# A larger allowance between engines in the list schedule of a Fourier, MoE and channel-mix kernel

## The chip, the cores and the metric

The kernel runs on one core of a Trainium2 chip. The time is microseconds (us) of device time of one execution. TensorE (PE in the profile) multiplies matrices into PSUM; VectorE (DVE) and ScalarE (ACT) do everything elementwise; SyncE (SP) and GpSimd (POOL) only start DMAs here. The program gives each engine its own list of instructions; an instruction that needs the result of another engine waits for a semaphore.

## The reference, cut to what matters

The input x has 4 batches of 3072 tokens with 256 channels, in float32.

```
X  = rfft(x, axis=1)
Yr = Xr @ w_r - Xi @ w_i + b_r ;  Yi = Xr @ w_i + Xi @ w_r + b_i
Y  = sign(Y) * max(|Y| - 0.01, 0)          (real and imaginary part apart)
x  = irfft(Y)                               stage 1
h  = x @ w_in ; x = (h - tanh(h)) @ w_out   stage 2, 256 -> 2048 -> 256
xk = mu_k*x + (1-mu_k)*x_prev ; xr likewise with mu_r
k  = max(xk @ w_k, 0) ; v = (k*k) @ w_v     stage 3, 256 -> 1024 -> 256
out = sigmoid(xr @ w_r2) * v
```

## The kernel before

Every float32 operand of a matmul is cut into a high and a low part, and each product is three matmuls: high by high, low by high, high by low. The cut costs one ScalarE copy (L345) and one VectorE subtraction (L348) for each tile.

Stage 1 does the transform in two steps per batch, with a trip through DRAM between them: first-step matmuls into PSUM banks `a`, 12 units per batch that take `q` tiles back from DRAM, a matmul into bank `g`, one into bank `y` with the weights, the threshold on VectorE (L529 to L534), the cut into `zh` and `zl`, a matmul into bank `v`, and so on.

Stage 2 goes over 24 chunks of 512 tokens and, within a chunk, 8 pieces of the hidden width (`reg_pair`, "a pair" below). The first matmul of a pair is done with seven products of half size instead of eight (`reg_h`). Two of the banks named `g` take three of them: ScalarE copies each result out (`p2`, `p5`, `p3`, L796). The other four go, one after the other, into one bank named `y` or `a` in turn (`m` in the code): each product adds to what the bank already holds, and after each of the first three an add on VectorE (L799, `hs<-y,p` or `hs<-a,p`) reads the bank. So the next product into that bank may only start when the add before it has read. Then ScalarE makes tanh (L839), VectorE subtracts (L840), both cut the result into `gh` and `gl` (L345, L348), and PE takes these with 6 matmuls of 512 columns for each half into the two banks `v`. Two banks stand behind each name, so PE always has several pairs under way.

Stage 3 goes over the 24 chunks again (`reg_m2`): four pieces of the same seven-product form, all with bank `y` for `m`; the square on VectorE (L968) or ScalarE; 12 matmuls of 256 columns for each piece into `v`; and four groups of 6 matmuls into bank `a` for the gate (`a<-wh,yh` and so on), each read by a sigmoid on ScalarE (L1003).

None of this is in the order in which the loops stand. The code only registers operations with an engine, a duration by formula, a priority and what they depend on; `_Plan.run` then makes a list schedule on a clock of its own, and the instructions are emitted in the order of the planned starts. On each engine the planner takes, among the operations that are ready at that time, the one of lowest priority number, and an operation is ready when all that it depends on have ended, plus an allowance where the other operation ran on another engine:

```
        for x in lst:
            if gated:
                t = o.start + 1e-3
            elif x.eng == o.eng == "pe":
                t = o.end
            else:
                t = o.end + o.lat
```

The allowance `o.lat` is `SEM` for everything but DMAs. It is in nanoseconds and only shapes the order: no instruction waits for it on the chip. The planner's durations for what is spoken of below are 3 x 119 for a product, `n * 1.042 + 69` for a VectorE operation with two inputs of n columns (336 for an add of 256), `n * 0.833 + 93` for a ScalarE operation from SBUF.

Of the kernel before, what the change touches and what calls it, by code (L numbers as in the profile page):

```python
# [142 lines left out]
    __slots__ = ("eng", "dur", "lat", "emit", "deps", "prio", "creates", "users", "nleft", "start", "end", "idx", "ready", "frees", "nbytes")  # L143


SEM = 130


class _Plan:
# [5 lines left out]

    def op(self, eng, dur, emit, prio, writes=(), reads=(), after=(), lat=SEM, seq=True, nbytes=0):
        o = _Op()
        o.nbytes = nbytes
        o.eng, o.dur, o.emit, o.prio, o.lat = eng, dur, emit, prio, lat
        o.idx = len(self.ops)  # L160
        o.start = o.end = None
        deps = set(after)
        o.creates, o.frees = [], []
        for t in reads:
            deps.update(t.writers)
            t.readers.append(o)
        for t in writes:
            if not t.writers:
                o.creates.append(t)
                if t.tag is not None:  # L170
                    self.rings.setdefault((t.pool, t.tag), []).append(t)
            elif seq:
                deps.add(t.writers[-1])
            else:
                deps.add(t.writers[0])
            t.writers.append(o)
            deps.update(r for r in t.readers if r is not o)
        for t in list(reads) + list(writes):
            if t.pool is not None:
                t.pool.ops.append(o)  # L180
        deps.discard(o)
        o.deps = deps
        self.ops.append(o)
        return o
# [867 lines left out]
```

## Time and profile before

| | us |
|---|---|
| median of 3 runs | 2008.94 |
| the three runs | 2005.75 to 2009.99 |
| the profiled execution | 2006.93 |
| its span, first to last instruction | 2005.1 |
| PE busy in the span | 1961.8 |
| VectorE busy | 1599.4 |
| ScalarE busy | 1476.9 |

The profiled execution lies 2.0 below the median of the runs. Stage 1 takes the first 350 us or so, stage 2 goes to about 1400, stage 3 to the end. PE is the engine that is nearly always busy, so the table alone says little of where time is lost. The end of a matmul is modelled in the profile and matmuls overlap (rows of 0.28 us start 0.12 apart), so a busy PE may still start its matmuls late. What tells it is the distance between the starts of neighbouring matmuls, and the length of a row: a matmul that was held up inside PE shows a longer row than its neighbours of the same shape.

### The profile page before, as it was taken

How to read it: one execution, taken by the hardware profiler on the slowest of the kernel's cores; microseconds unless marked ns; L12 is line 12 of the kernel's file. 1: busy time of each engine (PE TensorE's matmuls, PEld its weight loads, DVE VectorE, ACT ScalarE, POOL GpSimd, SP SyncE). 2: the span in 40 equal slices, each digit the busy share in tenths (PEclk: the TensorE clock that was granted, in tenths of full speed). 3: DMA queues.
4: the chain of work that ended last, by engine and by line, in shares of the span. 5: the costliest groups of instructions: out<-in, count | busy, mean ns of one | idle time of the engine just before them, and what ended most of it. 6: DMA issues, size and time to landing. Idle time of an engine off the chain costs nothing.

```text
span 2005.1 us, 36620 instructions
## 1 busy us (share of the span) xinstructions
PE 1961.8 (98%) x13760; PEld 1822.3 (91%) x13760; DVE 1599.4 (80%) x3107; ACT 1476.9 (74%) x3166; POOL 22.9 (1%) x42
## 2 busy tenths in 40 slices
PE   5999999999999999999999999999999999999998
PEld 3899989888888888888888888888999999999998
DVE  1688897788887878887878897779988888888885
ACT  3657566777777777777777787778877777777774
POOL 2000000000000000000000000000000000000000
PEclk8999999999999999999999999999999999999999
DMA  9699786511010101010101120001211111111101
GB/s 311 197 288 295 242 264 217 179 48 55 29 47 24 37 22 48 32 38 22 38 22 48 38 69 22 22 11 35 60 44 50 48 47 47 47 47 47 47 22 33
DMA packets 96194, 162.37 MB, mean 81 GB/s; under 512 B 11510, under 2 KB 56675, under 8 KB 96016
## 3 DMA queue, kind: packets, MB, share of 16 engines
q1 hardware_dynamic: 91008, 142.95, 22.8%
q0 software_dynamic: 4112, 13.93, 2.4%
q10 hardware_dynamic: 896, 3.15, 0.4%
q8 instruction: 108, 1.77, 0.4%
q14 instruction: 70, 0.57, 0.1%
HBM read 90.52 MB, written 69.47 MB: 80 GB/s over the span
## 4 chain that ended last, share of the span: by engine, by line
PE 89%; DVE 5%; DMA 3%; ACT 2%; issue 1%; SPq 0%; ACTq 0%; DVEq 0%
PE v L319 39%; PE y L319 20%; PE g L319 17%; PE a L319 14%; DVE hs L840 1%; DVE hs L799 1%; DVE yl L348 1%; DMA x<-in_x_dram 1%; DMA adr<-at 1%; DVE gl L348 1%; DMA ydr<-yt 0%; DMA out_dram<-ob 0%; DVE zl L348 0%; DMA vp<-vdr 0%; DMA yr<-ydr 0%
## 5 line engine op out<-in xcount | busy, mean ns | idle before, releaser
L345 ACT ACTIVATE gh<-hs 128x512 fp32r<-128x512 f32 x504 | 317.2, 629 | 139.2 <-PE v L319 131.4
L348 DVE TENSOR_TENSOR gl<-hs,gh 128x512 fp32r<-128x512 f32 x504 | 345.1, 685 | 79.5 <-ACT gh L345 79.1
L796 ACT ACTIVATE p<-g 128x256 f32<-128x256 f32 x864 | 318.7, 383 | 92.8 <-PE g L319 75.0
L840 DVE TENSOR_TENSOR hs<-hs,th 128x512 f32<-128x512 f32 x384 | 264.4, 689 | 122.1 <-ACT th L839 115.1
L319 PE MATMUL v<-gh,wl 128*128 128x512 f32 x768 | 303.6, 395 | 0.0
L319 PE MATMUL v<-gh,wh 128*128 128x512 f32 x768 | 303.3, 395 | 0.0
L319 PE MATMUL v<-gl,wh 128*128 128x512 f32 x768 | 300.0, 391 | 0.0
L839 ACT ACTIVATE th<-hs 128x512 f32<-128x512 f32 x384 | 241.5, 630 | 76.2 <-DVE hs L799 71.6
L799 DVE TENSOR_TENSOR hs<-y,p 128x256 f32<-128x256 f32 x588 | 241.4, 420 | 37.1 <-PE y L319 25.8
L319 PE MATMUL v<-ah,gh 128*128 128x256 f32 x768 | 217.5, 283 | 0.5 <-DVE ob L1004 0.5
L319 PE MATMUL v<-al,gh 128*128 128x256 f32 x768 | 217.3, 283 | 0.0
L319 PE MATMUL v<-ah,gl 128*128 128x256 f32 x768 | 217.3, 283 | 0.0
L319 PE MATMUL g<-yh,ah 128*128 128x256 f32 x648 | 183.2, 283 | 0.1
L319 PE MATMUL g<-yh,al 128*128 128x256 f32 x648 | 182.8, 282 | 0.0
L319 PE MATMUL g<-yl,ah 128*128 128x256 f32 x648 | 182.5, 282 | 0.0
L319 PEld LDWEIGHTS v<-gl,wh 128*128 128x128 f32 x768 | 144.4, 188 | 33.4
L319 PEld LDWEIGHTS v<-gh,wh 128*128 128x128 f32 x768 | 145.2, 189 | 18.1
L319 PEld LDWEIGHTS v<-gh,wl 128*128 128x128 f32 x768 | 145.2, 189 | 16.0
L319 PE MATMUL y<-yh,ah 128*128 128x256 f32 x496 | 149.8, 302 | 2.6 <-ACT hs L824 1.0
L319 PEld LDWEIGHTS v<-ah,gh 128*128 128x128 f32 x768 | 147.4, 192 | 0.8 <-DVE ob L1004 0.7
L319 PEld LDWEIGHTS v<-al,gh 128*128 128x128 f32 x768 | 147.4, 192 | 0.0
L319 PEld LDWEIGHTS v<-ah,gl 128*128 128x128 f32 x768 | 147.4, 192 | 0.0
(179 smaller groups left out, 4875.9 us busy)
## 6 DMA issues: line engine op xcount, KB each, us to landing
x<-in_x_dram SPq DMA_DIRECT2D x32, 384.0 KB, 5.2
q<-adr SPq DMA_DIRECT2D x48, 256.0 KB, 5.8
vdr<-v SPq DMA_DIRECT2D x48, 256.0 KB, 3.6
vp<-vdr SPq DMA_DIRECT2D x32, 384.0 KB, 6.3
ydr<-yt SPq DMA_DIRECT2D x64, 192.0 KB, 4.5
yr<-ydr SPq DMA_DIRECT2D x24, 512.0 KB, 4.0
xdr<-x SPq DMA_DIRECT2D x24, 512.0 KB, 3.1
xs<-xdr SPq DMA_DIRECT2D x20, 608.0 KB, 4.3
```

Source lines behind the costliest of these rows:

```text
L319: pe.matmul(out=o, lhsT=l, rhs=r, start=st, stop=en, **kw)
L345: op("act", c_act(n, psum), lambda: act.activation(out=o[1](), in_=i[1](), func=ACTF.Copy), prio, [o[0]], [i[0]])
L348: op("dve", c_dve(n), lambda: dve.tensor_tensor(out=o[1](), in0=i[1](), in1=h[1]().bitcast(F32), op=ALU.subtract), prio, [o[0]], [i[0], h[0]])
L796: op("act", c_act(HK, True), lambda: act.activation(out=o(), in_=p()[:, 0:HK], func=ACTF.Copy), prio, [o], [p])
L799: op("dve", c_dve(HK), lambda: dve.tensor_tensor(out=t()[:, half * HK:half * HK + HK], in0=p()[:, 0:HK], in1=s(), op=ALU.add), prio, [t], ...
L839: op("act", c_act(CK, False), lambda th=th, hs=hs: act.activation(out=th(), in_=hs(), func=ACTF.Tanh), z0, [th], [hs])
L840: op("dve", c_dve(CK), lambda th=th, hs=hs: dve.tensor_tensor(out=hs(), in0=hs(), in1=th(), op=ALU.subtract), z0, [hs], [th])
```

## The change

The allowance that the planner puts between an operation and one on another engine that waits for it goes from 130 to 210. Durations, priorities, buffers and the instructions are as they were; only their order on each engine can differ.

```
@@ -143,7 +143,7 @@
-SEM = 130
+SEM = 210
```

The order differs nearly everywhere. Three places show how.

PE in stage 2, at the same chunk and piece. First as it was: the last matmul of a product into bank `a_11168`, two products into `g` banks, and the next product into `a_11168`.

```order
L319 MATMUL a_11168<-yl_10260,ah3_4453 128x256
L319 MATMUL g_11273<-yh_10783,ah0_3741 128x256
L319 MATMUL g_11273<-yh_10783,al0_3748 128x256
L319 MATMUL g_11273<-yl_10795,ah0_3741 128x256
L319 MATMUL g_11279<-yh_10783,ah0_3741 128x256
L319 MATMUL g_11279<-yh_10783,al0_3748 128x256
L319 MATMUL g_11279<-yl_10795,ah0_3741 128x256
L319 MATMUL a_11168<-yh_10253,ah3_4453 128x256
```

And as it is now; the bank is called `a_11163` here, and `a_11287` is the bank of the next pair.

```order
L319 MATMUL a_11163<-yl_10263,ah3_4435 128x256
L319 MATMUL g_11273<-yh_10791,ah0_3685 128x256
L319 MATMUL g_11273<-yh_10791,al0_3715 128x256
L319 MATMUL g_11273<-yl_10795,ah0_3685 128x256
L319 MATMUL g_11279<-yh_10791,ah0_3685 128x256
L319 MATMUL g_11279<-yh_10791,al0_3715 128x256
L319 MATMUL g_11279<-yl_10795,ah0_3685 128x256
L319 MATMUL a_11287<-yh_10791,ah0_3685 128x256
L319 MATMUL a_11287<-yh_10791,al0_3715 128x256
L319 MATMUL a_11287<-yl_10795,ah0_3685 128x256
L319 MATMUL a_11163<-yh_10259,ah3_4435 128x256
```

The first product of the next pair has moved in between: there are three products now, not two, between one product into the bank and the next.

VectorE in stage 2, at the end of another pair. As it was (`hs0` and `hs1` are the two halves of a pair, `th` the tanh, `gl2` a low part):

```order
L799 TENSOR_TENSOR hs0_7568<-a_7502,p3_7520 128x256
L840 TENSOR_TENSOR hs0_7568<-hs0_7568,th_7589 128x512
L348 TENSOR_TENSOR gl2_7603<-hs1_7485,gh2_7594 128x512
L799 TENSOR_TENSOR hs1_7609<-a_7502,p5_7500 128x256
L348 TENSOR_TENSOR gl2_7622<-hs0_7510,gh2_7611 128x512
```

And now, the same pair with bank `a_7491`:

```order
L799 TENSOR_TENSOR hs0_7568<-a_7491,p3_7533 128x256
L348 TENSOR_TENSOR gl2_7597<-hs1_7481,gh2_7588 128x512
L840 TENSOR_TENSOR hs0_7568<-hs0_7568,th_7599 128x512
L799 TENSOR_TENSOR hs1_7611<-a_7491,p5_7513 128x256
L348 TENSOR_TENSOR gl2_7619<-hs0_7504,gh2_7605 128x512
```

The low part of an older pair has moved ahead of the subtraction that waits for tanh.

PE in stage 3, the gate of one chunk (`wh24`, `wl24` are its weights; each bank `a` is read by a sigmoid, and there are two of them). As it was, three gate groups in a row:

```order
L319 MATMUL a_18429<-wh24_14291,yh_18135 128x256 x2
L319 MATMUL a_18429<-wl24_14361,yh_18135 128x256 x2
L319 MATMUL a_18429<-wh24_14291,yl_18155 128x256 x2
L319 MATMUL a_18443<-wh24_14291,yh_18135 128x256 x2
L319 MATMUL a_18443<-wl24_14361,yh_18135 128x256 x2
L319 MATMUL a_18443<-wh24_14291,yl_18155 128x256 x2
L319 MATMUL a_18455<-wh24_14291,yh_18135 128x256 x2
L319 MATMUL a_18455<-wl24_14361,yh_18135 128x256 x2
L319 MATMUL a_18455<-wh24_14291,yl_18155 128x256 x2
```

And now, the second and the third of them with what lies between:

```order
L319 MATMUL a_18417<-wh24_14341,yh_18133 128x256 x2
L319 MATMUL a_18417<-wl24_14350,yh_18133 128x256 x2
L319 MATMUL a_18417<-wh24_14341,yl_18155 128x256 x2
L319 MATMUL y_18335<-ah3_17817,ah0_16678 128x256
L319 MATMUL y_18335<-ah3_17817,al0_16682 128x256
L319 MATMUL y_18335<-al3_17837,ah0_16678 128x256
L319 MATMUL y_18342<-ah3_17817,ah0_16678 128x256
L319 MATMUL y_18342<-ah3_17817,al0_16682 128x256
L319 MATMUL y_18342<-al3_17837,ah0_16678 128x256
L319 MATMUL a_18443<-wh24_14341,yh_18133 128x256 x2
L319 MATMUL a_18443<-wl24_14350,yh_18133 128x256 x2
L319 MATMUL a_18443<-wh24_14341,yl_18155 128x256 x2
```

Two products now stand between the second and the third group.

## Rows read from the trace of the kernel before

**Rows 1.** The page: busy us (share of the span) and instructions of each engine
```profile
PE 1961.8 (98%) x13760; PEld 1822.3 (91%) x13760; DVE 1599.4 (80%) x3107; ACT 1476.9 (74%) x3166; POOL 22.9 (1%) x42
```
**Rows 2.** Windows of stages 2 and 3: busy us (instructions), granted clock, DMA, GB/s
```profile
600.00:650.00 50.00, 50.00 (x308) 44.59 (x307) 38.67 (x74) 37.50 (x80) 0.00 (x0) 1.00 0.08 24
...
1500.00:1550.00 50.00, 50.00 (x414) 49.75 (x413) 42.51 (x85) 39.40 (x87) 0.00 (x0) 1.00 0.18 47
```
**Rows 3.** Waits: engine, line, waited for: us in total, times, longest
```profile
PEld y L319 <- DVE hs L799: 11.3, 44, 0.5
...
PEld a L319 <- DVE hs L799: 8.7, 34, 1.4
...
PE v L319 <- ACT zh L345: 5.2, 4, 2.5
```
**Rows 4.** PE groups, 400 to 1400 us: xcount, busy us, mean ns, idle
```profile
L319 PE MATMUL y<-yh,ah 128*128 128x256 f32 x371 | 111.7, 301 | 1.1 <-DVE hs L799 0.2
L319 PE MATMUL a<-yh,ah 128*128 128x256 f32 x368 | 110.2, 300 | 1.1 <-DVE hs L799 1.1
...
L319 PE MATMUL y<-yh,al 128*128 128x256 f32 x371 | 104.4, 281 | 0.0
...
L319 PE MATMUL a<-yh,al 128*128 128x256 f32 x368 | 103.5, 281 | 0.0
```
**Rows 5.** PE groups, 1400 to 1998 us
```profile
L319 PE MATMUL a<-wh,yh 128*128 128x256 f32 x192 | 41.0, 295 | 0.6 <-ACT sg L1003 0.6
...
L319 PE MATMUL a<-wh,yl 128*128 128x256 f32 x192 | 38.5, 282 | 0.0
L319 PE MATMUL y<-yh,ah 128*128 128x256 f32 x96 | 28.8, 300 | 0.3 <-DVE hs L799 0.3
L319 PE MATMUL y<-ah,ah 128*128 128x256 f32 x96 | 28.4, 295 | 0.2 <-DVE hs L799 0.2
L319 PE MATMUL y<-ah,ahk 128*128 128x256 f32 x96 | 28.1, 293 | 0.0
...
L319 PE MATMUL y<-ah,al 128*128 128x256 f32 x96 | 27.1, 282 | 0.0
L319 PE MATMUL y<-yh,al 128*128 128x256 f32 x96 | 27.1, 282 | 0.0
...
L319 PE MATMUL y<-ah,alk 128*128 128x256 f32 x96 | 27.1, 282 | 0.0
```
**Rows 6.** Timeline around 921 us, stage 2: start, us, engine, instruction
```profile
920.41 0.28 PE L319 MATMUL a<-yl,ah 128*128 128x256 f32 x1
...
920.74 0.42 DVE L799 TENSOR_TENSOR hs<-a,p 128x256 f32<-128x256 f32 x1
...
921.13 0.28 PE L319 MATMUL g<-yl,ah 128*128 128x256 f32 x1
921.21 0.19 PEld L319 LDWEIGHTS a<-yh,ah 128*128 128x128 f32 x1
921.25 0.35 PE L319 MATMUL a<-yh,ah 128*128 128x256 f32 x1
...
921.44 0.28 PE L319 MATMUL a<-yh,al 128*128 128x256 f32 x1
...
921.55 0.28 PE L319 MATMUL a<-yl,ah 128*128 128x256 f32 x1
```
**Rows 7.** Timeline around 618 us, stage 2
```profile
617.38 0.28 PE L319 MATMUL a<-yl,ah 128*128 128x256 f32 x1
...
617.68 0.69 DVE L840 TENSOR_TENSOR hs<-hs,th 128x512 f32<-128x512 f32 x1 [0.70 <-ACT th L839]
...
618.29 0.68 DVE L348 TENSOR_TENSOR gl<-hs,gh 128x512 fp32r<-128x512 f32 x1
...
619.08 0.42 DVE L799 TENSOR_TENSOR hs<-a,p 128x256 f32<-128x256 f32 x1
...
619.58 0.37 PE L319 MATMUL a<-yh,ah 128*128 128x256 f32 x1
```

## The prediction

> **What bounds the kernel now.** I read the page first: PE is busy for 1961.8 of 2005.1 us, VectorE for 1599.4, ScalarE for 1476.9 [rows 1]. Then the windows: in stages 2 and 3 PE is busy for all 50.00 us of a window at a granted clock of 1.00, and VectorE for 38.67 and 42.51 [rows 2]. So PE sets the pace there, and only an earlier start of its matmuls can save time; by busy time nothing is left to save. But ends of matmuls are modelled, so I turned to the length of the rows. A matmul that follows freely starts 0.12 us after the one before and shows 0.28 (921.13 to 921.25, 921.44 to 921.55); the one at 921.25 shows 0.35, and its successor starts 0.19 later [rows 6]. That is 0.07 us lost inside a PE that counts as busy. Grouped by kind, the reader sees where: the first matmul of a product (`yh,ah`) averages 301 and 300 ns, the second (`yh,al`) 281, with the same count [rows 4]. The surplus of busy time, 111.7 - 104.4 and 110.2 - 103.5, is 7.3 + 6.7 = 14.0 us for stage 2. The waits name the cause: weight loads for banks `y` and `a` wait for `hs`, the adds of L799 [rows 3]. In stage 3 the same subtraction gives 1.7 + 1.3 + 1.0 = 4.0 us for the products into `y` and 41.0 - 38.5 = 2.5 us for the gate [rows 5].
>
> On headroom, the Trainium skill (Perfetto Trace Analysis, "Identifying the Most-Contended Engine") says that matmul busy time misleads and that the weight loads' busy share should be used. By that rule a window of stage 2 with 44.59 of 50 would leave a tenth of the stage, some 100 us. The trace agrees with the first half alone: the starts and row lengths show 14.0 us in that stage, and I go by them.
>
> **Why the products are late, and what 210 does.** At 921 us the last matmul of a product into the bank ends at 920.69 (920.41 + 0.28), the add starts at 920.74 and ends at 921.16, the weight load starts at 921.21, and the matmul, due at 921.25, is 0.07 late [rows 6]. From the start of that last matmul the next one could follow freely at about 0.91 (0.84 + 0.07). The planner ends the product one matmul step after that start, at 0.12, and adds allowance, 0.336 for the add, allowance: 0.72 with 130, 0.88 with 210. Two products between put the matmul at 0.12 + 6 x 0.12 = 0.84, which the old allowance lets pass and the new one doesn't. The next possible place is three products, 1.20, which is ample.
>
> The order bears this out. Counting neighbouring products into one `y` or `a` bank with just two products between: 88 in stage 2 and 60 in stage 3 before, 1 and 0 now. Third gate groups right behind two others: 21 before, 1 now. The first and third fence of the change show one of each.
>
> **Part by part**, against the profiled execution, 2006.93 us:
> - Stage 2, two-product distances: 88 x 0.07 = 6.2 us saved. What is late next is nothing on that bank: the three-product distance leaves 0.29 us over.
> - Stage 3, products: between nothing and the 4.0 us of surplus. With 60 such distances, which at 0.07 would make 4.2, and none now, I take 4.0.
> - Stage 3, gate: 0 to 2.5 us; two products now stand where the third group waited for its sigmoid. I take 2.0.
> - Stage 2, the other 14.0 - 6.2 = 7.8 us. Here the distance on PE was wide enough, but the add came late on VectorE. At 617.66 (617.38 + 0.28) the product is done; VectorE runs the subtraction from 617.68 (it had idled 0.70 for tanh), then a low part from 618.29, and only at 619.08 the add; PE's matmul at 619.58 shows 0.37, 0.09 too long [rows 7]. In VectorE's list the sequence subtraction, low part, add stands 79 times before and 11 times now; the second fence shows a swap that lets the low part fill the idle time before the subtraction. That speaks for up to 7.8 us. Against it: stretches of four or more vector instructions between two adds grow from 50 to 79, and if each of the 29 new ones cost PE an average wait of weight loads into `a`, 8.7 / 34 = 0.26 [rows 3], that is 7.5 us lost. Between -7.5 and 7.8 I take 3.0, nearer the gain since rows 7 show the very sequence that goes.
> - Stage 1: the matmuls `v<-zh` lose 5.2 us in 4 waits on ScalarE's `zh` [rows 3], at the start and the ends of batches, where PE has little else. In the new order a `g` group is put between the first `v` groups (v, g, v, g, v, g for v, v, g, g, v, g), and at the last batch boundary three `y` halves, not two, stand between the last `a` group and the next `g` group. But everything there has moved, the SP list of DMA starts too (stores of `wdr`, loads of `q` and `vp` change places), and I can't price it from rows: between -5.2 and 5.2. I take 1.5.
> - The start (PE's list is the same up to the first `v` groups) and the end (`v` groups only, then the last four results): 0.
>
> Sum: 6.2 + 4.0 + 2.0 + 3.0 + 1.5 = 16.7 us, which gives 1990.2 on the profiled execution's scale. That execution lies 2.0 below the median of the runs, so on theirs it is 1992.2; I forecast 1991.
>
> The waits of `v` groups on `gh` and `gl` add no term: in the new order a half of a pair stands, but for the first pairs, at least 5.6 us of PE work (at 0.12 us for 256 columns and twice that for 512) behind the product that it needs, mostly over 8.8; before it was at least 7.8. The three vector steps of that chain take 0.42 + 0.69 + 0.68 = 1.8 us [rows 7].
>
> **Rivals.**
> 1. Nothing is gained: the lost 0.07 us are a pace that something else sets, and return elsewhere. For it: the same small gap recurs through both stages. Against it: PE is busy in the whole window while VectorE has 11.33 us of 50 free [rows 2], and after each wait the row says which add it waited for. If only a fourth of the direct 12.2 us comes through, the time is about 2004 to 2009; with none, 2006.9 on one scale, 2008.9 on the other. The Trainium skill (Perfetto Trace Analysis, "Optimization Strategy") says that consistent bubbles can mean too few buffers in SBUF or PSUM; a change of order alone would then save nothing. The trace speaks against it here: the bank that is waited for is one that the product itself goes on filling, and a third bank would not free it.
> 2. Slower: VectorE's list. PE now often runs two `v` groups back to back, then several products, so adds come in bunches and queue behind subtractions and low parts in VectorE's order. The price is 0.26 us each. It decides from the point where some 20 / 0.26 = 77 new waits eat up what the forecast's terms without stage 1 could bring at most (6.2 + 4.0 + 2.0 + 7.8 = 20.0); with 100 of the 192 pairs paying one, the time is 2006.9 - 20.0 + 26.0 = 2013. For it: the 29 longer stretches. Against it: those are 29, not 77, and the sequence that made the adds late has all but gone. The Trainium skill (TensorE: Matmul & The Clock Gate, "Architectural detail") calls VectorE's queue strictly first in, first out while PE may pull weight loads ahead; the add at 619.08 agrees, standing 1.4 us after its product with the low part before it [rows 7].
> 3. All of it: every late add goes and stage 1's 5.2 too. 6.2 + 4.0 + 2.5 + 7.8 + 5.2 = 25.7 us, or 1981.
>
> **How the numbers follow.** The forecast, with the direct terms and a part of the others, 1984 to 2001: 0.70. All of it: 0.10. Nothing, or so little that it is 2001 to 2010: 0.13, of which about 0.05 is still faster. Slower by the vector list or by stage 1: 0.07. From no change one can tell about 0.2% here, 4 us. So faster 0.85, same 0.08, slower 0.07. The range goes from 1981 to 2003, which leaves out about 0.06 below and 0.14 above.
>
> **What would show it.** In the changed kernel's groups, `yh,ah` into `y` and `a` in stage 2 should fall from 301 and 300 ns to under 290, and the gate's `wh,yh` from 295 to about 283. Weight loads that wait for `hs` should fall from 78 to under 40. The timeline should show adds that follow their product within half a microsecond where the low part now comes first. PE's stretch from 400 us to the end should shrink by 12 to 20 us, with stage 1 within 5 of before. I am wrong if those means fall and the time doesn't (rival 1), if the 0.28 us rows grow in another group, `g<-yh,ah` or `v<-gh,wh`, or if the waits on `hs` become fewer but longer (rival 2).

## The result and the profile after

| | before, us | after, us |
|---|---|---|
| median | 2009.06 (5 runs, 2005.75 to 2011.58) | 1987.15 (5 runs, 1984.03 to 1989.14) |
| the profiled execution | 2006.93 | 1989.14 |
| its span | 2005.1 | 1987.2 |

The changed kernel takes 0.9888 of the time before, with a 95% interval from 0.9873 to 0.9902. It is 1.1% faster; 1991 was forecast, within 1981 to 2003.

Three matmuls that both kernels have cut the span into its stages: the first product of stage 2, the first `v` matmul of stage 3 and the last matmul. In the timeline of before (start, duration, what ran):

```profile
348.91 0.28 PE L319 MATMUL g<-yh,ah 128*128 128x256 f32 x1
...
1409.33 0.28 PE L319 MATMUL v<-ah,gh 128*128 128x256 f32 x1
...
1997.93 0.28 PE L319 MATMUL v<-ah,gl 128*128 128x256 f32 x1
```

And in that of after:

```profile
352.01 0.28 PE L319 MATMUL g<-yh,ah 128*128 128x256 f32 x1
...
1397.56 0.28 PE L319 MATMUL v<-ah,gh 128*128 128x256 f32 x1
...
1980.10 0.28 PE L319 MATMUL v<-ah,gl 128*128 128x256 f32 x1
```

Stage 1 became 3.1 us longer in this pair, stage 2 went from 1060.4 to 1045.6, 14.9 shorter (the rows are rounded), and stage 3 from 588.6 to 582.5, 6.1 shorter. That is the whole gain of 17.9 us of span. The stages overlap on PE, so a cut says where a product starts and not how much work lies before it.

The page of after has PE busy for less time, with the same matmuls, and for the same share of the span as before [rows 1]:

```profile
PE 1946.2 (98%) x13760; PEld 1820.2 (92%) x13760; DVE 1596.3 (80%) x3107; ACT 1463.4 (74%) x3166; POOL 23.2 (1%) x42
```

So 15.6 of the 17.9 us came out of PE's busy time and only 2.3 out of its idle time. The windows say the same: PE is busy for all 50.00 us as before [rows 2], and has 315 matmuls in that time where it had 308, and 419 where it had 414. In stage 2 that is only a rough measure, since matmuls of 512 columns start 0.23 us apart and not 0.12, and their share differs from window to window.

```profile
600.00:650.00 50.00, 50.00 (x315) 45.13 (x314) 39.67 (x77) 38.18 (x83) 0.00 (x0) 1.00 0.09 29
1500.00:1550.00 50.00, 50.00 (x419) 50.00 (x418) 42.67 (x84) 38.56 (x86) 0.00 (x0) 1.00 0.17 46
```

Where it came out is seen in the groups by kind. In stage 2, 400 to 1400 us of after (busy time and mean ns behind the count), the first matmul of a product no longer stands above the second. The surplus of 14.0 us [rows 4] is (106.6 - 107.1) + (103.2 - 103.9) = -1.2, so it is gone. The 1.1 + 1.1 us of idle time that stood before the two first matmuls in [rows 4] are 0.0 as well:

```profile
L319 PE MATMUL y<-yh,al 128*128 128x256 f32 x379 | 107.1, 283 | 0.0
L319 PE MATMUL y<-yh,ah 128*128 128x256 f32 x379 | 106.6, 281 | 0.0
L319 PE MATMUL a<-yh,al 128*128 128x256 f32 x368 | 103.9, 282 | 0.0
...
L319 PE MATMUL a<-yh,ah 128*128 128x256 f32 x368 | 103.2, 280 | 0.0
```

In stage 3, 1400 to 1980 us of after, the same holds for the gate, whose first matmul had 295 ns, and for the products, which had 293 to 300 [rows 5]:

```profile
L319 PE MATMUL a<-wh,yh 128*128 128x256 f32 x188 | 38.2, 285 | 0.5 <-ACT sg L1003 0.3
L319 PE MATMUL a<-wh,yl 128*128 128x256 f32 x188 | 37.9, 283 | 0.0
L319 PE MATMUL y<-ah,ah 128*128 128x256 f32 x96 | 27.5, 286 | 0.3
...
L319 PE MATMUL y<-yh,ah 128*128 128x256 f32 x93 | 26.6, 286 | 0.4 <-DVE hs L799 0.4
```

The waits of weight loads on `hs` are nearly gone from the whole span: 78 before [rows 3], 8 now. On the other side of the bank, the adds of L799 wait more often for a product into `y` and less for one into `a`. Before:

```profile
DVE hs L799 <- PE y L319: 25.8, 52, 1.5
...
DVE hs L799 <- PE a L319: 18.4, 38, 0.6
```

And after:

```profile
DVE hs L799 <- PE y L319: 72.1, 96, 2.1
...
DVE hs L799 <- PE a L319: 5.6, 28, 1.0
...
PEld y L319 <- DVE hs L799: 3.5, 8, 0.8
```

One place of the new order, at the products of the change's first fences (timeline of after):

```profile
916.40 0.28 PE L319 MATMUL a<-yl,ah 128*128 128x256 f32 x1
...
916.72 0.42 DVE L799 TENSOR_TENSOR hs<-a,p 128x256 f32<-128x256 f32 x1
...
917.24 0.28 PE L319 MATMUL a<-yh,ah 128*128 128x256 f32 x1
...
917.60 0.28 PE L319 MATMUL a<-yh,ah 128*128 128x256 f32 x1
```

The product into the bank has its last matmul at 916.40, and the add has read the bank at 917.14. The row at 917.24 is the next pair's product, which has been put in between; only the one at 917.60 takes the same bank again, 1.20 us after the last, and shows 0.28 where it showed 0.35 [rows 6].

### The profile page after: what moved, and what is told of

It reads as the page before. It is cut to its first block, busy times and chain, and to the rows that moved or that the text cites. A ratio compares the mean times of both kernels' runs of the same rounds, so it can differ in the third digit from the quotient of the medians.

```text
span 1987.2 us, 36546 instructions
## 1 busy us (share of the span) xinstructions
PE 1946.2 (98%) x13760; PEld 1820.2 (92%) x13760; DVE 1596.3 (80%) x3107; ACT 1463.4 (74%) x3166; POOL 23.2 (1%) x42
## 4 chain that ended last, share of the span: by engine, by line
PE 92%; DMA 3%; DVE 3%; ACT 1%; issue 1%; ACTq 0%; SPq 0%; DVEq 0%
PE v L319 41%; PE y L319 19%; PE g L319 17%; PE a L319 14%; DMA adr<-at 1%; DMA raw<-in_moe_w_out_dram 1%; DMA out_dram<-ob 0%; DMA raw<-in_moe_w_in_dram 0%; DVE hs L799 0%; DMA q<-adr 0%; DMA ws<-wdr 0%; DVE x L923 0%; DVE zl L348 0%; DVE t L534 0%; DVE hs L968 0%
## 5 line engine op out<-in xcount | busy, mean ns | idle before, releaser
L799 DVE TENSOR_TENSOR hs<-y,p 128x256 f32<-128x256 f32 x588 | 244.3, 422 | 83.5 <-PE y L319 72.1
L319 PEld LDWEIGHTS v<-gh,wl 128*128 128x128 f32 x768 | 145.4, 189 | 17.8
L319 PE MATMUL y<-yh,ah 128*128 128x256 f32 x496 | 141.0, 284 | 1.6 <-DVE hs L799 1.5
```

The source lines that it names most:

```text
L319: pe.matmul(out=o, lhsT=l, rhs=r, start=st, stop=en, **kw)
L799: op("dve", c_dve(HK), lambda: dve.tensor_tensor(out=t()[:, half * HK:half * HK + HK], in0=p()[:, 0:HK], in1=s(), op=ALU.add), prio, [t], ...
```

## The experiments

In all of them only the allowances differ, so each has the same instructions in another order. "Surplus" is the busy time of the first matmuls of products into `y` and `a` less that of the second ones, in stage 2 (400 to 1400 us) and, with the gate, in stage 3 (1430 to 1960 us). "Two-product places" are those in PE's list with just two products between one product into a bank and the next. Before has 88 of them in stage 2 and 60 in stage 3. Each ratio is against runs of before that were taken together with that kernel's; their medians lie between 2007.8 and 2009.06, so medians of different kernels compare to about 1 us.

| | median, us (range) | ratio, 95% | two-product places, stages 2, 3 | surplus, stages 2, 3, us |
|---|---|---|---|---|
| before | | | 88, 60 | 14.0, 6.8 |
| after | 1987.15 (1984.03 to 1989.14) | 0.9888 (0.9873 to 0.9902) | 1, 0 | -1.2, 0.2 |
| 185 | 1996.71 (1989.92 to 1999.41) | 0.9936 (0.9924 to 0.9949) | 41, 28 | 2.1, 2.9 |
| 195 | 1985.56 (1983.5 to 1988.59) | 0.9886 (0.9873 to 0.9899) | 0, 0 | -0.6, 0.2 |
| 300 | 1986.44 (1984.04 to 1992.1) | 0.9893 (0.9877 to 0.991) | 0, 0 | -1.3, 0.3 |
| products and adds alone | 1988.83 (1988.19 to 1991.61) | 0.9904 (0.989 to 0.9918) | 0, 0 | 0.0, 2.4 |
| all but these | 1998.45 (1995.18 to 2011.26) | 0.9960 (0.9945 to 0.9974) | 105, 41 | 8.1, 2.3 |
| adds alone, 255 | 1991.27 (1988.16 to 1991.99) | 0.9913 (0.9897 to 0.9929) | 0, 0 | 1.0, 2.1 |
| by pairs of engines | 1994.18 (1986.82 to 2001.74) | 0.9925 (0.9906 to 0.9944) | 1, 0 | 1.0, 1.3 |
| 210 in stages 2 and 3 | 1987.03 (1983.78 to 1988.82) | 0.9890 (0.9876 to 0.9904) | 0, 0 | -0.3, 0.2 |
| 210 in stage 1 | 2009.67 (2004.95 to 2014.55) | 1.0006 (0.9997 to 1.0016) | 90, 60 | 14.1, 6.7 |
| 185 in stages 2 and 3 | 1990.45 (1989.97 to 1991.9) | 0.9913 (0.9898 to 0.9928) | 43, 28 | 2.2, 2.9 |
| 300 in stages 2 and 3 | 1998.44 (1996.09 to 2001.27) | 0.9954 (0.9938 to 0.997) | 0, 0 | -1.4, 0.3 |

**Is it a step, and where?** In the planner a product may return to its bank at twice the allowance plus 336 for the add, against 2 x 3 x 119 = 714 for two products. A step should lie between 185 (706) and 195 (726).

```
-SEM = 210
+SEM = 185
```

> Allowance 185 everywhere. Two allowances and the add make 2 x 185 + 336 = 706, under the 717 of two products, so the planner may still place them: its list has 41 two-product distances in stage 2 and 28 in stage 3 (88 and 60 at 130, 1 and 0 at 210), and 36 sequences subtraction, low part, add (79 and 11). Theory (each two-product distance costs 0.07 us, each such sequence 0.09): in stage 2 2.9 + 3.3 = 6.2 of the 14.0 us stay, in stage 3 about 2.5 of 6.5; gain some 11 us over before, about 1998, and the first matmul of a product in stage 2 stays at about 289 ns. Rival (time falls smoothly with the allowance): 55/80 of 21.9, a gain of 15, 1994.

With `SEM = 195` in the second kernel:

> Allowance 195 everywhere: 2 x 195 + 336 = 726, over 717. The list has no two-product distance in either stage, and 15 of the sequences subtraction, low part, add. Theory: nearly all of 210's gain, 1986 to 1991, first matmuls of products within 4 ns of the second ones. Rival (smooth): only 10 us of allowance more than 185, so some 3 us less than that kernel.

At 195 all is gained, at 185 two-product places are left, though only half of those of before: where the sum still lets the planner place two products, it often does otherwise. The groups of the kernel with 185, 400 to 1400 us, show what these cost:

```profile
L319 PE MATMUL y<-yh,ah 128*128 128x256 f32 x379 | 108.2, 285 | 0.0
L319 PE MATMUL y<-yh,al 128*128 128x256 f32 x379 | 106.8, 282 | 0.0
...
L319 PE MATMUL a<-yh,ah 128*128 128x256 f32 x368 | 104.2, 283 | 0.0
...
L319 PE MATMUL a<-yh,al 128*128 128x256 f32 x368 | 103.5, 281 | 0.0
```

That is 1.4 + 0.7 = 2.1 us, where 41 places at 0.065 make 2.7. So the two-product places are the whole surplus here. The two surpluses are 3.3 + 2.7 = 6.0 us above those of after, though, and this kernel is 9.6 behind it, so its time doesn't show the size of the step; what else it lost is told below.

**Which allowance does it?** First 210 behind the products and the adds of L799 alone, 130 elsewhere, then the complement.

```
-            op("pe", 3 * 119, e, prio, [o], [ah, al, yh, yl])
+            op("pe", 3 * 119, e, prio, [o], [ah, al, yh, yl], lat=210)
...
-            op("dve", c_dve(HK), ..., prio, [t], [p, s], seq=False)
+            op("dve", c_dve(HK), ..., prio, [t], [p, s], seq=False, lat=210)
```

> 210 only behind the products of the seven-product form and the adds of L799; 130 behind everything else. The list has 0 two-product distances but 37 sequences subtraction, low part, add. Stage 1 has none of these operations. Theory: in stage 3 the 6 us go, in stage 2 the 6.2 and more than half of the rest, and stage 1 is as before: a gain of 16 to 20 us, 1990 to 1993. Rival (the slack between ScalarE and VectorE is what helps, and the products' distance is a by-product): a gain under 8 us, over 2001.

> The complement: 130 behind the products and the adds, 210 behind everything else. The list has 105 two-product distances in stage 2, 41 in stage 3, and 25 of the sequences. Theory: in stage 2 105 x 0.07 + 25 x 0.09 = 9.6 of 14.0 us stay, in stage 3 some 2.7 of 4.0 for the products, the gate's 2.2 go; stage 1 is as with 210, which lost some 3 us there: a gain of 3 to 7 us, 2002 to 2006. Rival (slack between ScalarE and VectorE): a gain over 14 us, under 1995.

The two allowances alone take all of stage 2's surplus, and the time, 1988.83, is 1.2 us better than the best expected; what they leave is the gate (1.9 of the 2.4 in stage 3). The complement takes the gate (0.1 left) and leaves the two-product places, 105 of them. Its groups, 400 to 1400 us:

```profile
L319 PE MATMUL y<-yh,ah 128*128 128x256 f32 x375 | 110.7, 295 | 0.0
L319 PE MATMUL a<-yh,ah 128*128 128x256 f32 x368 | 106.9, 290 | 1.1 <-DVE hs L799 1.1
...
L319 PE MATMUL y<-yh,al 128*128 128x256 f32 x375 | 105.7, 282 | 0.0
...
L319 PE MATMUL a<-yh,al 128*128 128x256 f32 x368 | 103.8, 282 | 0.0
```

And one of the 105 places in its timeline, with the same row of 0.35 us as in [rows 6] and 0.18 to the next (0.19 there):

```profile
494.06 0.28 PE L319 MATMUL g<-yl,ah 128*128 128x256 f32 x1
494.18 0.35 PE L319 MATMUL a<-yh,ah 128*128 128x256 f32 x1
494.36 0.28 PE L319 MATMUL a<-yh,al 128*128 128x256 f32 x1
```

In stage 2 every such place is late, in every kernel that has them, by 0.065 to 0.067 us on the mean by the distances of starts. In stage 3 not all are: of the 60 of before 40 are late, of the complement's 41 about half. The complement's 1998.45 lies between what was expected, 2002 to 2006, and its rival, under 1995: 8.1 us of surplus are left in stage 2 and not 9.6, and nearly all of that is the 105 places (105 x 0.066 = 6.9). The waits at wider distances went here too.

**Is it the sum around the bank?** With 255 behind the adds alone (`lat=255` on the second line above, 130 on all else) the sum is 130 + 336 + 255 = 721, above 714, and the products keep their allowance.

> 255 behind the adds of L799 alone, 130 behind everything else, the products too. 130 + 336 + 255 = 721, over 717: no two-product distance, though the planner now starts the adds too early (it gives them 0.13 us after the product's planned end where the chip needs about 0.21) and frees PE too late. If only the sum round the bank matters, the same as with 210 behind both, 1986 to 1991. If the adds' start must be right too, because other vector work then stands before them, stage 2 keeps over 4 us of its waits, and it is over 1993.

The places are gone and 1.0 us of surplus stays. For that effect it doesn't matter on which side of the add the time is allowed. The time is just above the expected range; 1.9 of the 2.1 us left in stage 3 are the gate, whose allowance stays at 130.

**Does more cost something?** `SEM = 300`, to set the VectorE list against the distance on PE:

> Allowance 300. No two-product distance, but 88 sequences subtraction, low part, add (79 at 130, 11 at 210), and 155 stretches of four or more vector instructions between two adds (50, 79). If such a sequence costs 0.09 us wherever it stands, stage 2 loses 88 x 0.09 = 8 us again, 1995 and with the long stretches up to 2015. If it only costs where the product stands too near, nothing comes back, 1987 give or take stage 1's 3 us.

```profile
L319 PE MATMUL y<-yh,al 128*128 128x256 f32 x379 | 107.1, 283 | 0.0
L319 PE MATMUL y<-yh,ah 128*128 128x256 f32 x380 | 106.9, 281 | 0.0
```

In its stage 2 the two means are alike, as in after. Its VectorE list has the sequence subtraction, low part, add 88 times (before 79, after 11), and 155 stretches of four or more vector instructions between two adds (before 50, after 79). Neither costs anything that the surplus or the time shows.

**By pairs of engines**: 210 from PE, 180 into PE, 130 between ScalarE and VectorE. (Where an operation waits for a buffer to come free, the planner still counts 130 in this kernel.)

```
-                        t = o.end + o.lat
+                        t = o.end + (o.lat if o.nbytes else ALLOW.get((o.eng, x.eng), SEM))
```

> Allowances by the distances that the trace of before shows, counted from the planner's ends: 210 from PE to ScalarE or VectorE, 180 from these to PE, 130 between ScalarE and VectorE. One two-product distance in stage 2, none in stage 3, 14 sequences. Theory: stages 2 and 3 as with 210 within 3 us, stage 1 by its own order, which can go either way by 3: 1984 to 1990. Rival (slack between ScalarE and VectorE helps by itself): over 1995.

The surpluses are small, as the places are gone, but the runs spread over 15 us, and the median missed its expectation. The profile is of one of the faster runs, 1990.49; its stages 2 and 3 took 1046.2 and 582.6 us, like those of after. Where the slower runs lost their time is not shown.

**Stage 1 apart.** The planner takes its allowance from a variable that is set anew where stage 2 begins: in the first kernel 130 and then 210, in the second 210 and then 130.

```
-SEM = 210
+SEM = 130
+LATER = 210
...
+        o.lat = self.sem if lat is None else lat
...
+    plan.sem = LATER
     P2 = 3000.0
```

> 210 for all that is registered for stages 2 and 3, 130 for stage 1 (its conversions of weights too). Counts in the list are those of 210: no two-product distance, 12 sequences subtraction, low part, add. If stage 1 really lost some 3 us of the gain, because of its order, this is about 3 us faster than the changed kernel, 1983 to 1985; if that loss was a chance of one profile or a matter of where stage 2 begins, it is the same, 1987.

> The complement: 210 for stage 1, 130 for stages 2 and 3; 90 and 60 two-product distances, 81 sequences. Theory: nothing of the gain, and stage 1's loss: 2009 to 2013. Rival (stage 1 gained too, and the profile of the changed kernel misleads): under 2007.

Stages 2 and 3 bring all of it. What 210 does in stage 1 is not told from nothing: 1.0006, or between 0.6 us faster and 3.2 us slower. The 3.1 us that stage 1 lost in the profiled pair lie within that. Nor is that loss one of the order in stage 1 alone: in the profile of the second kernel stage 2 starts at 344.63, 4.3 us before that of before, and then takes 1066.0 us, 5.6 longer. A few us move between the two stages with the order, and the cut between them doesn't price either.

Then `LATER = 185` and `LATER = 300` with `SEM = 130` for stage 1: the first to see whether stage 1 or its passage to stage 2 had set the time of 185 that didn't fit, the second whether 300 is better still there:

> 185 for stages 2 and 3, 130 for stage 1. Two-product distances as with 185 everywhere: 43 in stage 2, 28 in stage 3. If that kernel's 1996.7 came from the passage between stages 1 and 2, where its profile lost some 10 us at half the granted clock, and the distances cost only their 43 x 0.063 + 28 x 0.062 = 4.4 us, this one comes out 4 to 5 us over the kernel with 210 there, 1990 to 1992. If the distances carry the whole difference, it stays at 1996 to 1998.

> 300 for stages 2 and 3, 130 for stage 1: no two-product distance, 87 sequences subtraction, low part, add. In the profile of 300 everywhere, stage 3 lost 2.4 us less than with 210, stage 2 the same. If that holds, 1983 to 1986, the best of all; if what stage 1 leaves to chance is larger than that, the same as 210, 1987.

With the same allowance in stages 2 and 3 as the kernel with 185 throughout, the first is 6.3 us faster (4.6 by the ratios) and has a spread of 2 us. It is as far behind 210 in stages 2 and 3, 3.4 us by medians and 4.6 by the ratios, as its places make it (4.4 by the count in its expectation). So the step between 185 and 195 is worth some 4 us, and what 185 gains over before, some 17 us, is the larger part. With the same as the kernel with 300 throughout, the second is 12 us slower, against the expectation, which held it for the best of all. The surpluses are those of their partners to 0.1 us, so the differences lie elsewhere. The profiles show one in the passage from stage 1 to stage 2. The windows there of 185 throughout (behind the busy times of the five engines stands PE's granted clock):

```profile
360.00:370.00 10.00, 8.11 (x45) 7.14 (x44) 9.01 (x18) 7.58 (x17) 0.00 (x0) 0.79 1.00 271
370.00:380.00 10.00, 10.00 (x49) 10.00 (x49) 3.27 (x7) 4.61 (x10) 0.00 (x0) 0.50 0.70 200
380.00:390.00 10.00, 10.00 (x63) 9.42 (x63) 5.49 (x12) 5.83 (x14) 0.00 (x0) 0.85 0.45 137
```

And of after:

```profile
360.00:370.00 10.00, 8.34 (x52) 6.45 (x52) 8.79 (x20) 8.64 (x21) 0.00 (x0) 1.00 1.03 266
370.00:380.00 10.00, 9.76 (x85) 9.55 (x85) 7.25 (x15) 6.65 (x15) 0.00 (x0) 1.00 1.03 297
380.00:390.00 10.00, 10.00 (x84) 9.74 (x84) 5.17 (x10) 7.22 (x17) 0.00 (x0) 1.00 0.56 202
```

PE is busy in both, but in the one the clock stands at 0.50 of full speed, the 1.2 GHz level, from 370 to 380, and 49 + 63 = 112 matmuls start in the 20 us, against 169. The 57 that are missing make 57 x 0.12 = 7 us. The kernel with 300 in stages 2 and 3 has 49 and 61 matmuls in those two windows and also a granted clock of 0.50.

## Why the prediction was right

**Start distances instead of busy time.** Right. PE's busy share was 98% before and after, and the surplus of the first matmuls was what there was to gain: it said 14.0 us for stage 2 and 6.5 for stage 3, and the stages became 14.9 and 6.1 shorter. Together that is 21.0, a little more than the 12 to 20 us that the prediction named as a sign for PE's stretch from 400 us on.

**Two-product places, 6.2 us, and stage 3's products, 4.0.** Right in mechanism, and in size for stage 2. The last places go at the step that the planner's sum gives, between 185 and 195; each costs 0.066 us in stage 2, where 0.07 was taken, so the 88 made 5.9 us; and the complement, which keeps them, keeps their cost. In stage 3 the sum of 60 x 0.07 = 4.2 hid that 20 of the 60 were not late and the other 40 showed 0.083 too much on the mean; together that is 3.6 us of row surplus.

**The gate, 2.0 us.** Right in size by luck; the place was wrong. The prediction had the third of three groups in a row wait for its sigmoid. With 210 on products and adds alone, third groups in a row fall from 21 to 1 in the list, and still 1.9 us of the gate's surplus stay. In before, the 21 third groups make 0.5 of the 2.5 us. The rest is the first group of a chunk, late by some 0.09 us in 19 of the 24 chunks. One chunk in before (two matmuls to a row, 0.40 where they start freely; the first, second and third group):

```profile
1660.39 0.64 ACT L1003 ACTIVATE sg<-a 128x256 f32<-128x256 f32 x2
...
1660.82 0.50 PE L319 MATMUL a<-wh,yh 128*128 128x256 f32 x2
...
1661.62 0.40 PE L319 MATMUL a<-wh,yh 128*128 128x256 f32 x2
...
1662.34 0.43 PE L319 MATMUL a<-wh,yh 128*128 128x256 f32 x2
```

The first group shows 0.10 too much and the third 0.03. By the order of the two lists, the sigmoids at 1660.39 are the last two of the chunk before, and the first of them reads the bank that the first group takes: it ends 0.06 us ahead of that group's start. After and the complement have 3 late gate groups each, before has 26. So the allowance on all but products and adds took away mostly this wait for a sigmoid of the chunk before; on which of those operations it acts is not shown.

**The wider distances in stage 2, 3.0 us of at most 7.8.** Mis-sized: all of it went (14.0 less 5.9 of the places is 8.1). The reason given was too narrow as well. The sequence subtraction, low part, add did fall from 79 to 11, but 300 has 88 of them and no surplus, and 185 has 36 and none beyond its two-product places. The rows of before show what the 78 waits of [rows 3] were. The 74 of them in stage 2 last 0.17 us or more, and the two-product places are not among them: at the one of [rows 6] no such wait is shown. They are the wide places with a late add. Only in 22 of the 74 does the add stand behind the prediction's sequence of subtraction and low part. In 42 it stands right behind a subtraction that had waited for tanh, with no low part between them, as here in VectorE's timeline of before:

```profile
438.57 0.69 DVE L840 TENSOR_TENSOR hs<-hs,th 128x512 f32<-128x512 f32 x1 [0.79 <-ACT th L839]
439.18 0.42 DVE L799 TENSOR_TENSOR hs<-y,p 128x256 f32<-128x256 f32 x1
```

PE's rows of the same moment show the product that the add reads, one `v` half behind it, and the next product with its long row (of the six matmuls of the half, the first and the last):

```profile
438.18 0.28 PE L319 MATMUL y<-yl,ah 128*128 128x256 f32 x1
438.30 0.40 PE L319 MATMUL v<-gh,wh 128*128 128x512 f32 x1
...
439.46 0.39 PE L319 MATMUL v<-gl,wh 128*128 128x512 f32 x1
439.69 0.35 PE L319 MATMUL y<-yh,ah 128*128 128x256 f32 x1
```

VectorE idled 0.79 us for tanh while the add's product, finished at 438.46, came to stand behind it. In the complement and in adds alone, such waits of weight loads are 3 and 6, though subtractions that waited for tanh stand right ahead of an add 149 and 106 times there (119 before). So neither sequence alone makes the late add; it takes one of them at a wide place with little room. Why every larger allowance, on whichever edges, clears nearly all of them is not settled.

**Stage 1, 1.5 us gained.** Not borne out: 3.1 us lost in the profiled pair, and no difference that the runs tell from nothing with 210 in stage 1 alone.

**The sum.** 16.7 was forecast against the profiled execution, and 17.8 lie between the two profiled executions. That the two are so close is luck: stage 2 gave 14.9 where its two terms were 9.2, 5.7 more, and stage 1 lost 3.1 in this pair where 1.5 of gain was set, 4.6 less, and the two misses cancel. By medians the gain is 21.9, since after's profiled execution was its slowest run, 2.0 above its median, and before's lay 2.1 below its own. On that scale 5.2 us came beyond the 16.7, which is about what the wider distances were set too low. It stayed in the range of 1981 to 2003, which had allowed for them.

**The rivals.** Nothing gained, by a pace or by too few buffers (the rule in the Trainium skill, Perfetto Trace Analysis, "Optimization Strategy", that consistent bubbles can mean too few buffers): refuted, since the bubbles were consistent and a change of order alone took them out. Slower by bunched adds on VectorE: refuted by 300, with 155 long stretches and no surplus. All of it, 1981: it was right for stage 2, where the whole 14.0 went, and wrong for stage 1.

## What to carry to other kernels

Compare the allowances of a list scheduler with what the trace shows. Here, from the planner's end of a product to the add is 0.21 us (920.41 + 0.12 to 920.74), and from the add's end in the planner to the matmul (920.74 + 0.336 to the 921.25 + 0.07 of its late start) 0.24, where the planner had 0.13 for each. It need not be exact: 195, less than either, brings all that 210 does, since places on PE come in whole products, and 300 costs nothing in the surplus of stages 2 and 3. Look for what is lost inside a busy engine by the row lengths of the first matmul of each kind against the second, and count the places in the instruction list that have too little between them.

## What the runs showed of the hardware that was not expected

A single short passage can cost more than a term of the sum, by the clock. In the kernel with 185, PE's waits between 345 and 370 us sum to 6.4 us, with 300 in stages 2 and 3 to 5.2, in after to 3.1, and in all others to 3.1 or less. The longest, in both of the first, is for a tile that comes back from DRAM; in the timeline of 185:

```profile
364.79 2.77 PE L319 MATMUL a<-e_sb,vp 96*128 96x96 f32 x16 [1.67 <-DMA vp<-vdr]
```

Behind it the granted clock fell to 0.50 and came back only between 380 and 390, with PE busy all the while (windows above). After kept 1.00, though PE was busy for little more of 360 to 370 us, 8.34 against 8.11. The kernel with 185 in stages 2 and 3 had a short drop there, 0.83 over 360 to 370, and 1.00 again from 370. By the distances of starts from 345 to 400 us PE lost 16.8 us in the kernel with 185 and 15.3 in that with 300 in stages 2 and 3, against 3.0 to 5.8 in before, after and the rest: 10 us or more for the one passage. The two misfits are 6.3 and 12 us. That the passage made them is argued from one profile of each kernel, but the mean granted clock of each run goes with it. Of the six runs of 185, five at 0.987 to 0.990 took 1995.4 to 1999.4 us, and one at 0.992 took 1989.92. Of the complement's twelve, eight at 0.991 to 0.994 took 1995.2 to 1999.3, and four at 0.987 to 0.989 took 2005.4 to 2011.3. That these four lost their time at the same passage is not shown, since its profile is of one of the eight.
